# Seven block products for w_out times g, from batch 4 on

## The chip, the cores and the metric

The kernel runs on one core of one Trainium2 chip. That core has five engines with a queue each: TensorE (PE in the profile; its weight loads are listed apart as PEld), VectorE (DVE), ScalarE (ACT), GpSimd (POOL) and SyncE (SP), which here issues nearly all DMAs. An engine works off its own queue strictly in the order in which the program was written out, and waits at an instruction until the semaphores that it names are there. The metric is the device time of one execution in microseconds (us). The kernel before took 1190.68 us, the median of three runs (1190.14, 1190.68, 1194.91).

## What is computed

Two stages follow each other: attention with a sigmoid instead of a softmax, and a feed-forward layer on its output. With 8 batches of 12 heads, 448 positions and a head size of 64, cut to what matters:

```python
scores = scale * np.matmul(q, k.transpose(0, 1, 3, 2)) - np.log(S)
attn_out = np.matmul(1.0 / (1.0 + np.exp(-scores)), v)
x = attn_out.transpose(0, 2, 1, 3).reshape(3584, 768)
h = x @ w_in                                   # 768 x 2048
g = np.where(h >= 1, h, np.where(h <= -1, 0.0, (h + 1) ** 2 / 4.0))
out = g @ w_out                                # 2048 x 768
```

Everything arrives and leaves in float32.

## The kernel before, in words

**Precision.** TensorE is fed float16. Each float32 operand is scaled by a power of two and split into a high half (its float16 rounding) and a low half (what is left, again float16), and a product is the sum of three float16 matmuls: high times high, high times low, low times high. That is why every matmul loop has the inner loop `for wh, xh in ((0, 0), (0, 1), (1, 0))`.

**Stages.** The work goes batch by batch. For batch b there is an *up* stage (w_in times x, giving h, and from it g) and a *down* stage (w_out times g, giving the output). While the up and down stages of batch b run, the attention of batch b+1 is computed in small steps between them; batch 7, the last, has no attention beside it. Batch 0 and 1 also contain the loading, scaling and splitting of the weights.

**Up.** From batch 2 on, `up_blocks` computes h with seven products instead of eight of half-size blocks (a Strassen-type scheme): w_in, seen as 2 x 2 blocks, was combined once into seven blocks (`mix`, in batch 1, into the DRAM tile `blocks`), x is combined into seven blocks `xc` at the start of each batch, and seven products of 224 columns each are added up on VectorE into the four quarters of h. One index i stands for a pair of 128-row chunks of h, i and i + 8; there are eight of them, of 63 matmuls each. VectorE adds the quarters (L697, 128x224, five for each i); these additions also free the PSUM tiles in which the products stand.

**Bend.** `bend` turns a chunk of h into g: a Relu on ScalarE (L735), two operations on VectorE (L736, L737), the rounding to the high half on ScalarE (L738) and the low half on VectorE (L739). Each is 128x448, and there are two such chains for each i. The halves go to `ghl`.

**Down.** `down` multiplies the split w_out, which stays in SBUF as `w_out_sb`, by `ghl`: for each of six row chunks m, 16 chunks f times three matmuls of 448 columns (L758), 288 in all for a batch. VectorE scales the result out of PSUM (L768) and SP stores it (L770). From batch 2 on the f run in the order (0, 8), (1, 9), ..., so that the pair that the up stage finishes last is used last.

**What sets the order.** Python code emits the instructions unit by unit; `step` calls of the attention are spread evenly over the units of a batch. A scheduler then lists the instructions of each engine by priority and by its own estimate of when their operands are ready. What it wrote out is what the chip runs.

## Time and profile before

| | |
|---|---|
| median of 3 runs | 1190.68 us |
| the profiled execution's own time | 1187.38 us |
| its span (first to last instruction on the core) | 1185.7 us |
| granted TensorE clock, mean | 0.991 |
| TensorE busy | 1144.9 us (97%), 7662 matmuls |
| VectorE busy | 854.9 us (72%) |
| ScalarE busy | 697.6 us (59%) |
| GpSimd busy | 332.8 us (28%) |

Busy time is the time in which at least one instruction of the engine is under way. The up stage of batch b begins at about 394 us for batch 2, 532 for batch 3, 669 for batch 4, 806 for batch 5, 944 for batch 6 and 1078 for batch 7: a batch takes some 137 us, the last 108. In the timeline of an engine, instructions of one kind that follow each other are merged into one row with their count; in the table of groups each row has the mean duration of one. A duration includes the time in which the result drains, which the next instruction of the same engine overlaps if it doesn't depend on it.

### The profile page before, as it was taken

The page shows a single profiled execution, that of the slowest core. Times are in us where ns is not written, and L with a number is a line of the kernel's source. Part 1 is how long each engine was busy: PE and PEld are TensorE (multiplying, and loading weights), DVE is VectorE, ACT ScalarE, POOL GpSimd, SP SyncE. Part 2 cuts the span into 40 slices and gives each one's busy share as a digit, 9 for nine tenths or more (in the row PEclk, how much of TensorE's full clock was granted, in tenths as well). Part 3 has the DMA queues.
Part 4 walks back from the last instruction along what each step waited for, and adds up shares of the span by engine and source line. Part 5 has one row for each costly group of instructions (what it writes and reads, how often), then busy time and mean ns, then how long its engine had stood idle before and what let it go on. Part 6 is the DMA issues. An engine that isn't in the chain of part 4 may idle for free.

```text
span 1185.7 us, 20268 instructions
## 1 busy us (share of the span) xinstructions
PE 1144.9 (97%) x7662; PEld 669.3 (56%) x7662; DVE 854.9 (72%) x1828; ACT 697.6 (59%) x1158; POOL 332.8 (28%) x393
## 2 busy tenths in 40 slices
PE   5889899999999999999999999999999999999998
PEld 1224333444445776457754677557764577558954
DVE  6999999999956588457973689456884678736830
ACT  5886576665654577547864578455864476613510
POOL 3004410011323244234345235332532353310000
PEclk9899999999999999999999999999999999999999
DMA  9842354437542266224643065423552246302400
GB/s 367 322 153 76 118 161 152 134 119 257 182 148 72 95 217 210 76 72 142 238 163 102 30 236 208 135 64 128 204 211 64 65 147 220 126 24 87 163 16 32
DMA packets 58113, 170.01 MB, mean 143 GB/s; under 512 B 8608, under 2 KB 39840, under 8 KB 51872
## 3 DMA queue, kind: packets, MB, share of 16 engines
q1 hardware_dynamic: 56288, 159.29, 39.1%
q10 hardware_dynamic: 1728, 9.44, 2.2%
...
## 4 chain that ended last, share of the span: by engine, by line
PE 71%; DVE 17%; DMA 4%; ACT 3%; issue 2%; POOL 2%; SPq 0%; POOLq 0%; ACTq 0%; DVEq 0%
PE po L758 33%; PE ph L688 22%; PE pav L498 8%; PE psc L416 3%; PE psc L425 2%; PE ph L722 2%; DVE g L736 2%; PE psc L411 1%; DVE g L737 1%; DVE ghl L739 1%; DMA raw<-qkv 1%; DVE ahl L466 1%; DVE w_in_sb L244 1%; DVE mixa L632 1%; DVE w_out_sb L247 1%
## 5 line engine op out<-in xcount | busy, mean ns | idle before, releaser
L758 PE MATMUL po<-ghl,w_out_sb 128*128 128x448 f16 x2304 | 446.3, 353 | 1.5 <-DVE qkv_e L131 0.6
L758 PEld LDWEIGHTS <-w_out_sb 128*128 128x128 f16 x2304 | 221.7, 98 | 219.4 <-issue 15.9
L688 PE MATMUL ph<-w_in_sb 128*128 128x224 f16 x3024 | 307.7, 259 | 1.3 <-DVE g L737 0.9
L688 PEld LDWEIGHTS <-w_in_sb 128*128 128x128 f16 x3024 | 282.6, 98 | 30.1 <-issue 27.2
L466 DVE SCALAR_TENSOR_TENSOR ahl<-psc,ahl 128x896 f16<-128x896 f32 (+1 forms) x170 | 153.0, 900 | 105.7 <-ACT ahl L465 103.6
L378 POOL TENSOR_SCALAR raw<-raw,qkv_s 128x448 f32<-128x448 f32 (+1 forms) x93 | 71.0, 777 | 449.9 <-DVE qkv_i L139 346.3
L457 ACT ACTIVATE psc<-psc,nls,sqk 128x896 f32<-128x896 f32 (+1 forms) x136 | 129.5, 971 | 103.5 <-PE psc L425 86.6
L465 ACT ACTIVATE ahl<-psc 128x896 f16<-128x896 f32 (+1 forms) x170 | 126.9, 762 | 29.8 <-DVE ahl L466 28.6
L722 PE MATMUL ph<-xhl,w_in_sb 128*128 128x448 f16 x576 | 114.5, 356 | 4.7 <-DVE g L737 3.4
L344 ACT ACTIVATE dump<-raw 128x448 f16<-128x448 f32 (+1 forms) x105 | 61.9, 589 | 85.8 <-DMA raw<-qkv 84.5
L697 DVE TENSOR_TENSOR xhl<-ph,xhl 128x224 f32<-128x224 f32 x240 | 87.7, 383 | 25.3 <-PE ph L688 19.4
L738 ACT ACTIVATE ghl<-g 128x448 f16<-128x448 f32 x128 | 72.5, 573 | 44.2 <-DVE g L737 43.8
L498 PE MATMUL pav<-ahl,v 128*64 128x448 f16 x748 | 95.6, 360 | 0.0
L735 ACT ACTIVATE g<-xhl,hr,ihr 128x448 f32<-128x448 f32 x96 | 68.7, 752 | 41.9 <-DVE xhl L697 41.0
L722 PEld LDWEIGHTS <-w_in_sb 128*128 128x128 f16 x576 | 55.7, 99 | 63.6 <-issue 14.4
L736 DVE SCALAR_TENSOR_TENSOR g<-g,rk 128x448 f32<-128x448 f32 x112 | 81.4, 741 | 10.2 <-ACT g L735 10.0
L739 DVE TENSOR_TENSOR ghl<-g,ghl 128x448 f16<-128x448 f32 x128 | 85.0, 672 | 5.3 <-ACT ghl L738 4.8
L768 DVE TENSOR_SCALAR o<-po,od 128x448 f32<-128x448 f32 x48 | 32.5, 679 | 61.1 <-PE po L758 60.8
L380 POOL TENSOR_TENSOR hl<-raw,hl 128x448 f16<-128x448 f32 x62 | 71.1, 1167 | 0.0
L416 PE MATMUL psc<-qk 128*128 128x448 f16 x252 | 66.3, 354 | 2.0 <-ACT a L454 1.0
L737 DVE SCALAR_TENSOR_TENSOR g<-xhl,ihs,g 128x448 f32<-128x448 f32 x96 | 66.3, 708 | 0.3
L498 PEld LDWEIGHTS <-v 128*64 128x64 f16 x748 | 36.3, 109 | 37.9 <-issue 23.0
...
## 6 DMA issues: line engine op xcount, KB each, us to landing
w_in_sb<-blocks SPq DMA_DIRECT2D x48, 1344.0 KB, 6.1
...
```

What stands on the lines that cost most here:

```text
L416: nc.tensor.matmul(out, kq[:, j, 1, w], kq[:, j, 0, :], start=True, stop=False)
L457: nc.scalar.activation(a, a, AF.Sigmoid, bias=nls, scale=sqk)
L465: nc.scalar.activation(hi, x, AF.Copy, scale=ATT)
L466: nc.vector.scalar_tensor_tensor(out=lo, in0=x, scalar=ATT, in1=hi, op0=ALU.mult, op1=ALU.subtract)
L498: nc.tensor.matmul(pav[j * D : (j + 1) * D, :S], *terms[j][t], start=c == 0 and t == 0, stop=mid and t == len(terms[j]) - 1,)
L688: nc.tensor.matmul(out, w[:, wt, wh, c * P : (c + 1) * P], xc[:, xt, c, xh, :], start=j in (0, 2) and c + wh + xh == 0, stop=c == HC - 1 a ...
L697: add = lambda out, q, other: nc.vector.tensor_tensor(out=out, in0=quarter(q), in1=other, op=ALU.add)
L722: nc.tensor.matmul(ph[:, :S], w_in_sb[:, f, wh, c * P : (c + 1) * P], xhl[:, c, xh, :], start=c == 0 and wh + xh == 0, stop=c == NCC - 1 a ...
L736: nc.vector.scalar_tensor_tensor(out=g, in0=g, scalar=rt, in1=g, op0=ALU.min, op1=ALU.mult)
L737: nc.vector.scalar_tensor_tensor(out=g, in0=h, scalar=ihs, in1=g, op0=ALU.mult, op1=ALU.max)
L739: (nc.gpsimd if f % GPOOL else nc.vector).tensor_tensor(out=ghl[:, f, 1, :], in0=g, in1=hi, op=ALU.subtract)
L758: nc.tensor.matmul(po[:, :S], w_out_sb[:, f, wh, m * P : (m + 1) * P], ghl[:, f, gh, :], start=f == lo and wh + gh == 0, stop=f == hi - 1 ...
```

## The change

From batch 4 on (`SD = 4`) the down stage also uses seven products of half-size blocks.

- `mix_out` makes seven blocks from w_out, in eight pieces of two chunks each, with the same kind of arithmetic as `mix` (two sums and four combinations on VectorE, four roundings on ScalarE, four low halves and six rescalings on VectorE), and stores them in the DRAM tile `oblocks` by seven DMAs for each piece. It is emitted in batches 2 and 3.
- In the down stage of batch b >= 4 the blocks come back through a ring of six buffers of 512 KB each (128 x 2048 float16) that lie in the second part of `w_out_sb`, whose old contents aren't needed any more; one such load belongs to each product of 24 matmuls.
- `bend_blocks` takes the place of the two `bend` chains for an index i: Relu (128x896), two VectorE operations (128x896), four subtractions (128x224) that combine g into seven blocks, a rounding of 128x1568 on ScalarE and a low half of 128x1568 on VectorE. The blocks `gc` lie in the old `ghl` for i < 4 and in the first part of `w_out_sb` for i >= 4.
- `down_blocks` runs 3 x 7 products of eight chunks f times three matmuls of 224 columns, 504 in a batch, and adds the quarters of the result up on VectorE (L898 in the changed kernel, five for each m) and ScalarE.
- For m = 0 the first four products use the chunks f < 6 first (`ORD = 6`) and f = 6, 7 after that.
- Some constants move: four pairs of batch 7 have their largest values found by VectorE instead of ScalarE (`MAX_ACT` 47 to 43), two clamps of w_in in the first 30 us go from GpSimd to VectorE (`CLAMP`), two early loads are issued later (`L0`), the priority that the additions of the quarters get is smaller (`Q_PRIO` 72 to 12), and `mix` of w_in ends a little later (`MIX1`). Small tiles share buffers.

```diff
-MAX_ACT = 47
-L0 = 9
+MAX_ACT = 43
+L0 = 16
-CLAMP = 7
+CLAMP = 4
+SD = 4
+ORD = 6
+OMIX0 = 4
+OMIX1 = 96
+GP9 = 0
-MIX1 = 85
-Q_PRIO = 72
+MIX1 = 95
+Q_PRIO = 12
...
+    def mix_out(i):
...
+            (nc.gpsimd if r < MIXP else nc.vector).tensor_tensor(
+                out=a[:, r], in0=w_out_sb[:, chunk, 0, :], in1=w_out_sb[:, chunk, 1, :], op=ALU.add
+            )
+        a11, a21, a12, a22 = a[:, 0, :H], a[:, 0, H:], a[:, 1, :H], a[:, 1, H:]
+        nc.vector.scalar_tensor_tensor(out=a22, in0=a21, scalar=ratio, in1=a22, op0=ALU.mult, op1=ALU.add)
+        nc.vector.tensor_tensor(out=a21, in0=a11, in1=a21, op=ALU.subtract)
+        nc.vector.scalar_tensor_tensor(out=a11, in0=a11, scalar=minus, in1=a22, op0=ALU.mult, op1=ALU.add)
+        nc.vector.tensor_tensor(out=a12, in0=a12, in1=a11, op=ALU.subtract)
...
+        for t in range(4):
+            hi, scale = sv[:, t, :, 0, :], to[t != 1]
+            nc.scalar.activation(hi, src[:, t], AF.Copy, scale=scale)
+            nc.vector.scalar_tensor_tensor(
+                out=sv[:, t, :, 1, :], in0=src[:, t], scalar=scale, in1=hi, op0=ALU.mult, op1=ALU.subtract
+            )
...
+        for t in range(NB):
+            part = st[:, (t - 3) * DM : (t - 2) * DM] if t > 2 else pl[:, t * DM : (t + 1) * DM]
+            nc.sync.dma_start(
+                out=oblocks[:, t, :, i, :].rearrange("m p n -> p m n"), in_=part.rearrange("p (m n) -> p m n", m=HC)
+            )
...
-        if j == 6:
+        if j == 6 and b < SD:
             bend(b, i + NFC // 2, hg)
             bend(b, i, hf)
+        elif j == 6:
+            bend_blocks(b, i)
+
+    def bend_blocks(b, i):
...
+        nc.scalar.activation(g, h, AF.Relu, bias=hr, scale=ihr)
+        nc.vector.scalar_tensor_tensor(out=g, in0=g, scalar=rt, in1=g, op0=ALU.min, op1=ALU.mult)
+        nc.vector.scalar_tensor_tensor(out=g, in0=h, scalar=ihs, in1=g, op0=ALU.mult, op1=ALU.max)
+        sub = lambda o, x, y: nc.vector.tensor_tensor(out=t[:, o], in0=t[:, x], in1=t[:, y], op=ALU.subtract)
+        sub(4, 1, 0)
+        sub(1, 3, 1)
+        sub(5, 3, 4)
+        sub(6, 2, 5)
+        hi, lo = (gc[i][:, k].rearrange("p t n -> p (t n)") for k in range(2))
+        nc.scalar.activation(hi, blk, AF.Copy)
+        (nc.gpsimd if GP9 and i % GP9 == 1 else nc.vector).tensor_tensor(out=lo, in0=blk, in1=hi, op=ALU.subtract)
...
+    def down_blocks(b, m, j, lo, hi):
...
+        for f in range(lo, hi):
+            for wh, gh in ((0, 0), (0, 1), (1, 0)):
+                nc.tensor.matmul(
+                    out, w[:, f, wh, :], gc[f][:, gh, gt, :],
+                    start=j in (0, 2) and f + wh + gh == 0, stop=f == NHC - 1 and wh == 1, skip_group_check=True,
+                )
+        if hi < NHC:
+            return
+        load_block(n + RING)
...
+    def downs_blocks(b):
...
+        for m in range(HC):
+            late = 4 if m == 0 else 0
+            order += [(m, j, 0, ORD) for j in range(late)] + [(m, j, ORD, NHC) for j in range(late)]
+            order += [(m, j, lo, lo + NHC // 2) for j in range(late, NB) for lo in (0, NHC // 2)]
...
-        units = ups_blocks(b) + downs(b)
+        units = ups_blocks(b) + (downs(b) if b < SD else downs_blocks(b))
...
+                if 1 < b < SD:
+                    if b == 2 and u == 0:
+                        mix_scales(wo)
+                        omixed = 0
+                    v = (b - 2) * len(units) + u
+                    end = (SD - 3) * len(units) + OMIX1
+                    while omixed < NFC // 2 and v >= OMIX0 + omixed * (end - OMIX0) // (NFC // 2):
+                        mix_out(omixed)
+                        omixed += 1
```

How the scheduler's order moves is seen at three places.

**VectorE, start of batch 2's up stage.** `xhl<-ph` are the additions of the quarters, `ahl` the attention of the next batch, `xm` its maximum. Before:

```order
L697 TENSOR_TENSOR xhl<-ph,xhl 128x224
L466 SCALAR_TENSOR_TENSOR ahl<-psc,ahl 128x896
L508 TENSOR_REDUCE xm<-x_91 128x1
L697 TENSOR_TENSOR xhl<-ph,xhl 128x224 x2
L466 SCALAR_TENSOR_TENSOR ahl<-psc,ahl 128x896
L697 TENSOR_TENSOR xhl<-ph,xhl 128x224
L736 SCALAR_TENSOR_TENSOR g<-g,rk_3407 128x448
```

Now (`mixa`, `mixs` and `mixp` are tiles of `mix_out`):

```order
L711 TENSOR_SCALAR mixp<-w_out_sb,mixes 128x3x128 x6
L377 TENSOR_SCALAR sqk<-qkv_i 128x1
L378 TENSOR_SCALAR sqk<-qkv_i 128x1
L526 TENSOR_REDUCE xm<-x_91 128x1
L688 TENSOR_TENSOR mixa<-w_out_sb 128x768 x2
L484 SCALAR_TENSOR_TENSOR ahl<-psc,ahl 128x896
L765 TENSOR_TENSOR xhl<-ph,xhl 128x224 x3
L692 SCALAR_TENSOR_TENSOR mixa<-mixa,mixes 128x384
L765 TENSOR_TENSOR xhl<-ph,xhl 128x224
L693 TENSOR_TENSOR mixa<-mixa 128x384
```

The instructions of `mix_out` stand between the additions. Counted over the whole program, 70 of its 128 instructions on VectorE stand ahead of batch 2's first addition, beside the down stage of batch 1, and the other 58 between batch 2's first and last addition; none is left for the down stage of batch 2 or for batch 3.

**VectorE, end of batch 7's up stage.** Before, from the last two additions to the output:

```order
L697 TENSOR_TENSOR xhl<-ph,xhl 128x224 x2
L736 SCALAR_TENSOR_TENSOR g<-g,rk_11832 128x448
L736 SCALAR_TENSOR_TENSOR g<-g,rk_11822 128x448
L737 SCALAR_TENSOR_TENSOR g<-xhl,ihs_11836,g 128x448
L737 SCALAR_TENSOR_TENSOR g<-xhl,ihs_11826,g 128x448
L739 TENSOR_TENSOR ghl<-g,ghl 128x448 x2
L768 TENSOR_SCALAR o<-po,od 128x448 x6
```

Now:

```order
L765 TENSOR_TENSOR xhl<-ph,xhl 128x224 x2
L794 TENSOR_TENSOR blk<-blk 128x224
L801 TENSOR_TENSOR w_out_sb<-blk,w_out_sb 128x1568
L794 TENSOR_TENSOR blk<-blk 128x224 x3
L792 SCALAR_TENSOR_TENSOR blk<-blk,qm 128x896
L793 SCALAR_TENSOR_TENSOR blk<-xhl,ihs_12686,blk 128x896
L801 TENSOR_TENSOR w_out_sb<-blk,w_out_sb 128x1568
L794 TENSOR_TENSOR blk<-blk 128x224 x4
L801 TENSOR_TENSOR w_out_sb<-blk,w_out_sb 128x1568
L898 SCALAR_TENSOR_TENSOR u<-po,od,u 128x224 x2
```

After the last two additions there were six instructions until g was complete; now there are 13: a subtraction and the low half of i = 5, the rest of i = 6, and all of i = 7.

**VectorE, end of batch 4's up stage.** Before, from the last two additions to the last low half:

```order
L697 TENSOR_TENSOR xhl<-ph,xhl 128x224 x2
L736 SCALAR_TENSOR_TENSOR g<-g,rk_6844 128x448
L736 SCALAR_TENSOR_TENSOR g<-g,rk_6834 128x448
L737 SCALAR_TENSOR_TENSOR g<-xhl,ihs_6848,g 128x448
L737 SCALAR_TENSOR_TENSOR g<-xhl,ihs_6838,g 128x448
L156 CAST mb<-m_8178 128x3
L739 TENSOR_TENSOR ghl<-g,ghl 128x448 x2
```

Now, the last twelve rows up to the last low half:

```order
L792 SCALAR_TENSOR_TENSOR blk<-blk,qm 128x896
L153 TENSOR_SCALAR qkv_s<-qkv_e 128x3
L157 TENSOR_SCALAR qkv_i<-qkv_e 128x3
L801 TENSOR_TENSOR w_out_sb<-blk,w_out_sb 128x1568
L793 SCALAR_TENSOR_TENSOR blk<-xhl,ihs_7079,blk 128x896
L377 TENSOR_SCALAR sqk<-qkv_i 128x1
L378 TENSOR_SCALAR sqk<-qkv_i 128x1
L526 TENSOR_REDUCE xm<-x_91 128x1
L794 TENSOR_TENSOR blk<-blk 128x224
L484 SCALAR_TENSOR_TENSOR ahl<-psc,ahl 128x896 x2
L794 TENSOR_TENSOR blk<-blk 128x224 x3
L801 TENSOR_TENSOR w_out_sb<-blk,w_out_sb 128x1568
```

Ahead of these, behind the last two additions, stand three more subtractions, one `ahl` of 128x896 and one of 64x448, and two tiny ones. In batches 5 and 6 it reads alike. On TensorE, 30 matmuls of the down stage stand ahead of the last 18 of the up stage in each of batches 4 to 7, and 42 more of the chunks f < 6 behind them, before the first that needs f = 6.

More of the change, by code (lines that the diff above doesn't have):

```diff
@@ L123, in sigmoid_attention_mlp @@
     blocks = drm_p.tile([NFC // 2, P, SET], F16, name="blocks")
+    NHC = NFC // 2
+    GC, OB, RING = 2 * NB * HN, NHC * 2 * P, 6
+    gflat, oflat = (t.rearrange("p f h n -> p (f h n)") for t in (ghl, w_out_sb))
+    gc = [gflat[:, k * GC : (k + 1) * GC] for k in range(NHC // 2)]
+    gc += [oflat[:, k * GC : (k + 1) * GC] for k in range(NHC // 2)]
+    gc = [t.rearrange("p (h t n) -> p h t n", h=2, t=NB) for t in gc]
+    ring = [oflat[:, NHC // 2 * GC + k * OB : NHC // 2 * GC + (k + 1) * OB] for k in range(RING)]
+    ring = [t.rearrange("p (f h n) -> p f h n", f=NHC, h=2) for t in ring]
+    oblocks = drm_p.tile([HC, NB, P, NHC, 2 * P], F16, name="oblocks")
     def scales(m, n, tag, pool=None, square=False, less=0):
         pool = pool or sml_p
-        few = {"bufs": 1} if tag == "x" else {}
+        few = {"bufs": 1 if tag == "x" else 2} if pool is sml_p else {}
         mask, top = (EXP_MASK - EXP_ONE, TOP - 1) if square else (EXP_MASK, TOP - less)
-        e = sml_p.tile([P, 3], F32, tag="e", name=tag + "_e")[:, :n]
+        e = sml_p.tile([P, 3], F32, tag="e", name=tag + "_e", bufs=2)[:, :n]
         nc.vector.tensor_scalar(out=e, in0=m, scalar1=TINY, scalar2=None, op0=ALU.max)
@@ L617, in keep @@
             return t
-        low = keep("low", wi.scale[0], wi.scale[1], ALU.min, 0.25, ALU.mult)
-        keep("inv", wi.inv[0], wi.inv[1], ALU.max, 4.0, ALU.mult)
-        to = [keep("to%d" % k, low, wi.inv[k], ALU.mult) for k in range(2)]
-        keep("ratio", wi.scale[1], wi.inv[0], ALU.mult)
+        low = keep("low", w.scale[0], w.scale[1], ALU.min, 0.25, ALU.mult)
+        keep("inv", w.inv[0], w.inv[1], ALU.max, 4.0, ALU.mult)
+        to = [keep("to%d" % k, low, w.inv[k], ALU.mult) for k in range(2)]
+        keep("ratio", w.scale[1], w.inv[0], ALU.mult)
         keep("minus", mixed["ratio"], -1.0, ALU.mult)
@@ L649, in mix @@
         nc.sync.dma_start(out=blocks[i][:, 3 * DM :], in_=st)
[L650 removed]
+        pl = raw_p.tile([P, GC // 2], I32, tag="raww", name="mixp")[:, : 2 * DM].bitcast(F16)[:, : 3 * DM]
         pv = pl.rearrange("p (t h n) -> p h t n", t=3, h=2)
@@ L770, in down, with load_block, quarter @@
             nc.sync.dma_start(out=dst, in_=o)
+    OPRODUCTS = (0, 0, 0), (3, 5, 1), (4, 1, 2), (6, 4, 3), (1, 2, 0), (2, 6, 2), (5, 3, 3)
+    use = []
+    def load_block(n):
+        if n < HC * NB * (B - SD):
+            m, j = use[n % len(use)]
+            dst = ring[n % RING].rearrange("p f h n -> p (f h n)")
+            nc.sync.dma_start(out=dst, in_=oblocks[m, OPRODUCTS[j][0]].rearrange("p f n -> p (f n)"))
+    def down_blocks(b, m, j, lo, hi):
+        n = use.index((m, j)) + (b - SD) * HC * NB
+        if j % 2 == 0 and j < 4 and lo == 0:
+            hold["o", j] = ps_mo.tile([P, 512], F32, tag="mo", name="po")
+        if m == 0 and j == 0 and lo == 0:
+            hold["od"] = down_sc[b, None]()
+        if j == 0 and lo == 0:
+            hold["o"] = [out_p.tile([P, S], F32, tag="o", name="o%d" % r) for r in range(2)]
+            hold["u"] = tmp_p.tile([P, S], F32, tag="tmp", name="u")
+        wt, gt, q = OPRODUCTS[j]
+        def quarter(q):
+            return hold["o", q // 2 * 2][:, q % 2 * 256 : q % 2 * 256 + HN]
+        out, w = quarter(q), ring[n % RING]
+        for f in range(lo, hi):
[3 more added lines that the diff above has]
+                    start=j in (0, 2) and f + wh + gh == 0, stop=f == NHC - 1 and wh == 1, skip_group_check=True,
+                )
+        if hi < NHC:
+            return
+        load_block(n + RING)
+        o, od = hold["o"], hold["od"]
+        u2, u3 = hold["u"][:, :HN], hold["u"][:, HN:]
+        add = lambda out, q, other: nc.vector.scalar_tensor_tensor(
+            out=out, in0=quarter(q), scalar=od, in1=other, op0=ALU.mult, op1=ALU.add
+        )
+        with tc.high_priority(offset=Q_PRIO):
+            if j == 1:
+                nc.scalar.activation(u2, quarter(0), AF.Copy, scale=od)
+                add(u2, 1, u2)
+            elif j == 3:
+                add(u3, 2, u2)
+                add(o[1][:, HN:], 3, u3)
+            elif j == 4:
+                nc.scalar.activation(o[0][:, :HN], quarter(0), AF.Copy, scale=od)
+            elif j == 6:
+                add(o[1][:, :HN], 2, u2)
+                add(o[0][:, HN:], 3, u2)
+        if j == 6:
+            for r in range(2):
+                row = (m + r * HC) * P
+                nc.sync.dma_start(out=out_t[row : row + P, b * S : (b + 1) * S], in_=o[r])
@@ L901, in sigmoid_attention_mlp @@
         first = at
-        share = [DW if b < SB or u < len(units) - 48 else 8 for u in range(last)]
+        share = [DW if b < SB or u < len(units) - NDOWN else 8 for u in range(last)]
         share = [sum(share[:u]) / sum(share) for u in range(last + 1)]
@@ L924, in sigmoid_attention_mlp @@
                     block_scales(b + 1, inv_x)
+                if b == SD - 1 and u == len(units) - 1:
+                    downs_blocks(SD)
+                    for n in range(RING):
+                        load_block(n)
                 if b == 1 and u == last - 2:
```

65 lines of the change are left out of this document (49 added, 16 removed).

## The prediction

> **What bounds the kernel now.** First the page's busy times and slices:
>
> ```profile
> span 1185.7 us, 20268 instructions
> PE 1144.9 (97%) x7662; PEld 669.3 (56%) x7662; DVE 854.9 (72%) x1828; ACT 697.6 (59%) x1158; POOL 332.8 (28%) x393
> PE   5889899999999999999999999999999999999998
> DVE  6999999999956588457973689456884678736830
> ```
>
> TensorE is full from slice 5 on, so less matmul work shortens the run, as long as no other engine takes its place. VectorE is no flat 72%: it swings between 3 and 9 tenths inside each batch. So I cut the up stages out, from the first to the last addition of the quarters, for batches 2, 4 and 7, and then the last down stage (columns: stretch, its length, then busy us and instructions of each engine):
>
> ```profile
> core 0: us, PE busy (x) PEld busy (x) DVE busy (x) ACT busy (x) POOL busy (x), PEclk, DMA share, GB/s
> 397.50:469.00 71.50, 71.50 (x633) 54.61 (x632) 61.69 (x132) 54.44 (x97) 35.39 (x44) 1.00 0.55 191
> 671.80:743.90 72.10, 72.10 (x638) 55.04 (x636) 62.20 (x133) 54.70 (x98) 35.64 (x44) 1.00 0.55 190
> 1080.20:1132.40 52.20, 51.26 (x509) 48.59 (x508) 38.37 (x82) 22.41 (x45) 0.00 (x0) 1.00 0.36 134
> 1132.00:1185.70 53.70, 49.98 (x265) 25.64 (x262) 8.24 (x14) 2.56 (x4) 0.00 (x0) 1.00 0.07 26
> ```
>
> TensorE never idles in the two full batches, but VectorE has only 10 us to spare in 72: 61.69 of 71.50 and 62.20 of 72.10. The slack of VectorE lies in the down stages. The change takes work from TensorE in the down stages and gives work to VectorE in the up stages, where there is least room.
>
> **What TensorE saves.** Prices from batch 7, where nothing stands between the matmuls:
>
> ```profile
> 1100.59 25.19 PE L688 MATMUL ph<-w_in_sb 128*128 128x224 f16 x261 [0.94 <-DVE g L737]
> 1131.50 50.48 PE L758 MATMUL po<-ghl,w_out_sb 128*128 128x448 f16 x266
> ```
>
> A matmul of 448 columns takes 50.48 / 266 = 0.1898 us, one of 224 takes 25.19 / 261 = 0.0965 us. A down stage was 288 x 0.1898 = 54.7 us and becomes 504 x 0.0965 = 48.6 us: 6.0 us saved, in four batches **-24.1 us**.
>
> [...]
>
> **What VectorE gets.** Groups by shape (count, busy us, mean ns of one, idle before):
>
> ```profile
> L736 DVE SCALAR_TENSOR_TENSOR g<-g,rk 128x448 f32<-128x448 f32 x112 | 81.4, 741 | 10.2 <-ACT g L735 10.0
> L737 DVE SCALAR_TENSOR_TENSOR g<-xhl,ihs,g 128x448 f32<-128x448 f32 x96 | 66.3, 708 | 0.3
> L739 DVE TENSOR_TENSOR ghl<-g,ghl 128x448 f16<-128x448 f32 x128 | 85.0, 672 | 5.3 <-ACT ghl L738 4.8
> L697 DVE TENSOR_TENSOR xhl<-ph,xhl 128x224 f32<-128x224 f32 x240 | 87.7, 383 | 25.3 <-PE ph L688 19.4 <-ACT xhl L700 2.7 <-PE psc L159 2.7
> L632 DVE TENSOR_TENSOR mixa<-w_in_sb 128x768 f32<-128x768 f16 x16 | 14.7, 958 | 2.3 <-DMA blocks<-mixs 2.3
> L637 DVE SCALAR_TENSOR_TENSOR mixa<-mixa,mixes 128x384 f32<-128x384 f32 x8 | 4.9, 616 | 0.0
> L655 DVE TENSOR_SCALAR mixp<-w_in_sb,mixes 128x384 f16<-128x384 f16 x16 | 4.3, 314 | 0.0
> L466 DVE SCALAR_TENSOR_TENSOR ahl<-psc,ahl 128x896 f16<-128x896 f32 x102 | 110.7, 1085 | 97.8 <-ACT ahl L465 97.6
> L465 ACT ACTIVATE ahl<-psc 128x896 f16<-128x896 f32 x102 | 92.6, 913 | 0.6
> L738 ACT ACTIVATE ghl<-g 128x448 f16<-128x448 f32 x128 | 72.5, 573 | 44.2 <-DVE g L737 43.8
> ```
>
> *mix_out in batch 2.* The order puts 58 of its 128 VectorE instructions between batch 2's first and last addition: 6 of 128x768 (0.958), 13 combinations and 15 low halves of 128x384 (0.616) and 24 rescalings (0.314): 5.7 + 17.2 + 7.5 = 30.4 us; with one attention instruction fewer (1.085), 61.69 + 30.4 - 1.1 = 91.0 us of VectorE work. TensorE has 71.50 us there plus 17 matmuls of the down stage that moved ahead (17 x 0.19 = 3.2): 74.7. An in-order queue can't do 91 us of work in 74.7, and the additions that free the PSUM tiles stand behind the mix instructions, so TensorE waits: 16 us as the upper end. Durations contain drains which the next instruction overlaps (0.08 us each, by the pair of additions in the next fence: 0.69 for two of 0.383); 58 + some 50 existing ones take off 8.6. For the lower end, 4, some of the remaining lag is taken up behind the stretch, by the down matmuls that don't need the last chunks. I take **+10**, nearer to the sum without drains. The 70 instructions in the down stage of batch 1 cost nothing: VectorE has room there, and its cover is the 48 matmuls between two outputs; without it they would cost what the other 58 do.
>
> *bend_blocks.* An index i took 2 x (0.741 + 0.708 + 0.672) = 4.2 us of VectorE. By the slope from 448 to 768 columns (0.672 to 0.958, 0.9 ns each) an operation of 896 takes 1.14 and one of 1568 about 1.8; with four subtractions of 0.383: 2 x 1.14 + 1.5 + 1.8 = 5.6 us. In batches 4 to 6 the order leaves 10 us more of VectorE in the stretch: 62.2 + 10 = 72 against 74 on TensorE. That fits, barely; I take 0.5 us a batch, **+1.5** (0 to 6).
>
> *The end of the up stage.* This is where most is lost. Now, in batch 7 (TensorE as above: 18 matmuls end at 1131.66):
>
> ```profile
> 1131.70 0.69 DVE L697 TENSOR_TENSOR xhl<-ph,xhl 128x224 f32<-128x224 f32 x2 [2.41 <-PE ph L688]
> 1132.98 1.34 DVE L736 SCALAR_TENSOR_TENSOR g<-g,rk 128x448 f32<-128x448 f32 x2 [0.59 <-ACT g L735]
> 1134.23 1.27 DVE L737 SCALAR_TENSOR_TENSOR g<-xhl,ihs,g 128x448 f32<-128x448 f32 x2
> 1135.56 1.22 DVE L739 TENSOR_TENSOR ghl<-g,ghl 128x448 f16<-128x448 f32 x2
> ```
>
> g is complete 5.1 us after the last up matmul, under a down stage that can wait that long. In the changed order VectorE still has two additions (0.69), eight subtractions (8 x 0.34 with drains overlapped in part, 2.7), three low halves (5.4) and two operations of 896 (2.3), and waits for ScalarE's rounding of 1568 columns (0.573 + 1120 x 0.76 ns, the slope to L465's 913, = 1.4): 12.5 us. TensorE has 42 + 3 matmuls that don't need f = 7: 4.3 us. So it idles 8 us in batch 7, less if the low half of i = 5 starts before the last additions are due: **+7** (4 to 9). What was the saving of that batch is gone.
>
> In batches 4 to 6 VectorE's row is longer (three `ahl` of 1.085 and one of 64x448 come in: some 15.5 us), but TensorE has attention to do: 48 matmuls of 224 columns (4.6) and about 4.9 us of attention stand ahead of the first with f = 7. 15.5 - 9.5 = 6.0; some of it is the attention's own chain, which would run anyway, so I take 4.5 each (3 to 8): **+13.5**.
>
> *The rest.* The last addition pair is one addition longer than the single scaling before: **+0.4**. ScalarE: 54.7 of 72 us, and two chains become one: nothing. MAX_ACT moves four pairs' maxima to VectorE, under batch 5's and 6's down stage mostly; CLAMP and L0 touch the first 60 us, where VectorE gets two instructions and loses two waits: 0, within 2 us either way. Q_PRIO alone leaves batch 3's order as it was: 0.
>
> *The ring.* Each product of 24 matmuls (2.3 us) needs 512 KB.
>
> ```profile
> w_in_sb<-blocks SPq DMA_DIRECT2D x48, 1344.0 KB, 6.1
> ```
>
> At this row's 1344 KB in 6.1 us, 512 KB take 2.3 us, just the pace, with six buffers to smooth it: 0. If it is slower, TensorE waits in 84 products.
>
> **Sum.** -24.1 + 10 + 1.5 + 7 + 13.5 + 0.4 = +8.3 us. The profiled execution took 1187.38 us, 3.3 less than the median of the runs: 1187.4 + 8.3 + 3.3 = **1199 us**. All lower ends give -8.7 us (1182), all upper ends +33 (1224).
>
> **Rivals.** A change of 0.5% (6 us) is about what can be told from none.
>
> *Faster: the waits are hidden.* For it: TensorE kept on at full VectorE load in batch 1,
>
> ```profile
> 230.00:260.00 30.00, 27.55 (x137) 12.88 (x135) 29.66 (x64) 18.24 (x31) 4.67 (x3) 0.94 0.22 69
> 300.00:330.00 30.00, 29.64 (x165) 14.27 (x164) 29.80 (x52) 21.11 (x36) 10.77 (x11) 1.00 0.43 140
> ```
>
> losing 2.5 and 0.4 us in 30 with VectorE at 99%. If batch 2 costs 4, the ends of the up stages 2 in batches 4 to 6 and 2.5 in batch 7: -24.1 + 4 + 6 + 2.5 + 0.4 = -11 us, **1179 us**. Against it: there VectorE's demand equalled the time; in batch 2 it exceeds it. Chance 0.33.
>
> *No change.* The waits just eat the saving (7 + 10 + 6 + 1): **1190 us**, 0.17.
>
> *VectorE and GpSimd get in each other's way.* The longest and the usual low half (min/median/max ns) show it:
>
> ```profile
> L739 DVE TENSOR_TENSOR ghl<-g,ghl x128: 608/622/1572, 103.1 to 1136.2; 128x448 f16<-128x448 f32 x128
> ```
>
> If every instruction of bend_blocks (8 x 5.6 = 45 us) had to share its time with GpSimd's 35.6 us, a stretch would need 80 instead of 74 us: 4 to 6 us in each of batches 4 to 6, **1213 us**; the median at the minimum speaks for few such meetings. Chance 0.07. [...]
>
> *The ring comes late* in the down stages: at 2.6 us a load, 84 x 0.3 = 25 us, **1224 us**, 0.04.
>
> **Chances.** Forecast (slower, 1197 to 1209) 0.39. Faster 0.33, same 0.17, slower 0.39 + 0.07 + 0.04 = 0.50. Range 1176 to 1214, which leaves out the fast end of the faster case and the late ring; the forecast's own range is 1194 to 1209.
>
> **What would show it.** Right: down matmuls of 224 columns at 96 ns; VectorE above 95% in batch 2's up stage with TensorE waiting there some 10 us for additions (L765); gaps of TensorE ahead of L889 in four places, 4 to 8 us long, released by VectorE's L801 or ScalarE's L800; batch 3 as before. Wrong: TensorE without idle time in batch 2, or a first f = 7 matmul that follows at once.

## The result, and the profile after

The changed kernel takes **1264.0 us** (median of 4 runs, 1258.3 to 1265.6) against 1191.2 (1190.1 to 1194.9): 1.0597 times the time before, interval 1.0554 to 1.0639. The forecast was 1199, slower, with a range up to 1214: the sign was right, the size was not. The profiled execution took 1265.62 us, 78.2 more than the 1187.38 before.

Busy times and slices of the page, as shown of before in the prediction:

```profile
span 1263.9 us, 22469 instructions
PE 1161.5 (92%) x8526; PEld 757.4 (60%) x8526; DVE 988.6 (78%) x2008; ACT 724.2 (57%) x1126; POOL 351.6 (28%) x391
PE   4889899799989878999999999799888999799978
DVE  5999998898979989656873699657996579936951
PEclk9899899999989999999999999899998999999989
```

TensorE is no longer full: from slice 5 on there are holes of 1 to 3 tenths, most of them in slices in which VectorE shows 8 or 9, or just behind such, and its granted clock dips with some of them. To place the loss, both executions are cut at the first addition of the quarters in each batch's up stage (L697, now L765); the first row is all that lies ahead of batch 2's up stage, the last batch 7 to the end. Windows of before, with the columns of the prediction (stretch, length, busy us of TensorE, its weight loads, VectorE, ScalarE, GpSimd, then the granted clock):

```profile
0.00:397.50 397.50, 362.63 (x1827) 155.46 (x1828) 338.10 (x687) 254.62 (x394) 78.29 (x75) 0.97 0.49 169
397.50:534.90 137.40, 137.40 (x1023) 88.45 (x1022) 94.36 (x213) 86.81 (x151) 53.83 (x68) 1.00 0.42 143
672.10:809.40 137.30, 137.30 (x1025) 88.52 (x1023) 94.56 (x214) 86.73 (x152) 53.83 (x68) 1.00 0.42 143
809.40:947.30 137.90, 137.40 (x1023) 88.45 (x1021) 94.66 (x213) 86.66 (x151) 53.64 (x68) 1.00 0.42 143
947.30:1080.20 132.90, 132.12 (x985) 85.90 (x984) 92.43 (x195) 71.26 (x113) 39.09 (x46) 1.00 0.34 119
1080.20:1185.70 105.50, 100.84 (x770) 74.03 (x768) 46.23 (x94) 24.76 (x48) 0.00 (x0) 1.00 0.22 80
```

The same windows of the changed kernel (here with batch 3):

```profile
0.00:418.80 418.80, 373.76 (x1860) 159.56 (x1861) 375.32 (x766) 265.42 (x414) 77.69 (x73) 0.96 0.52 174
418.80:575.80 157.00, 142.66 (x989) 87.88 (x989) 122.56 (x273) 94.11 (x165) 56.34 (x68) 0.97 0.52 160
575.80:713.00 137.20, 137.20 (x1024) 88.52 (x1023) 93.76 (x206) 86.85 (x152) 54.21 (x68) 1.00 0.49 166
713.00:857.50 144.50, 136.40 (x1233) 108.35 (x1231) 113.42 (x229) 91.36 (x142) 59.83 (x69) 0.96 0.61 207
857.50:1010.80 153.30, 138.80 (x1239) 109.09 (x1237) 115.83 (x227) 84.93 (x123) 60.48 (x69) 0.97 0.59 200
1010.80:1151.30 140.50, 131.38 (x1181) 105.25 (x1179) 105.87 (x194) 73.27 (x96) 43.09 (x46) 0.98 0.55 187
1151.30:1263.90 112.60, 101.35 (x1014) 98.78 (x1012) 61.86 (x120) 28.30 (x37) 0.00 (x0) 0.97 0.47 158
```

Row by row: +21.3 before batch 2, +19.6 in batch 2, nothing in batch 3 (137.20, as before), then +7.2, +15.4, +7.6 and +7.1 in batches 4 to 7; together 78.2. So about half was lost before a single new product ran, where mix_out works and the changed constants act, and half in the four batches that were to save 24.1. In both halves VectorE's busy time is what grew: +37 and +28 us in the first two rows, some 19, 21, 13 and 16 in batches 4 to 7. In these four TensorE's busy time is as it was (507.9 us against 507.7), so the 24 saved came back in another form, and the time in which it is idle went from 5.9 to 43.0 us: that is the loss.

The up stages alone, first to last addition, of batches 2, 4, 5, 6 and 7:

```profile
418.80:511.20 92.40, 79.88 (x639) 56.65 (x639) 87.78 (x191) 63.43 (x113) 33.32 (x39) 0.96 0.66 206
713.00:792.40 79.40, 77.64 (x694) 58.84 (x692) 74.43 (x138) 59.00 (x89) 38.49 (x44) 1.00 0.55 197
857.50:942.40 84.90, 80.15 (x713) 60.70 (x710) 74.23 (x132) 56.80 (x86) 38.26 (x44) 1.00 0.56 196
1010.80:1093.60 82.80, 78.03 (x673) 57.25 (x670) 74.86 (x135) 52.80 (x68) 39.87 (x44) 0.98 0.48 168
1151.30:1205.10 53.80, 52.08 (x541) 51.60 (x540) 45.17 (x93) 21.57 (x28) 0.00 (x0) 1.00 0.44 157
```

Before, they were 71.5 us long in batch 2, 72.1 in batch 4 and 52.2 in batch 7 (the prediction's windows), with 62, 62 and 38 us of VectorE.

What TensorE waits for in batches 4 to 6 (713 to 1151.3 us) its groups show (count, busy us, mean ns of one, idle before and who ended it):

```profile
L756 PE MATMUL ph<-w_in_sb 128*128 128x224 f16 x1500 | 155.6, 260 | 3.7 <-DVE xhl L765 2.0 <-ACT xhl L774 1.6
L434 PE MATMUL psc<-qk 128*128 128x448 f16 x102 | 29.6, 364 | 10.3 <-DMA qk<-hl 9.2 <-DVE ahl L484 1.0
```

Of 31.7 us of such waits, 3.7 stand ahead of up products, for the quarters (L765, L774); 8.7 ahead of down products, for the last g (L800, L801); and 18.4, the most, ahead of the attention's matmuls, of which L434 is one. Before, it was 1.3 us in all.

The saving itself is there. The last down products (start, us, count; the first group takes 1.31 and the next starts 1.15 after it, so the pace is read from start to start):

```profile
1257.24 1.31 PE L889 MATMUL po<-ghl,w_out_sb 128*128 128x224 f16 x12
1258.39 1.31 PE L889 MATMUL po<-w_out_sb 128*128 128x224 f16 x12
```

12 matmuls of 224 columns in 1.15 us are 95.8 ns each; the 96.5 of the prediction stand, and 504 x 0.0958 = 48.3 us.

Last, the end of batch 7's up stage on TensorE (start, us, count, in brackets the idle time ahead and who ended it), and the clock there in windows of 2 us:

```profile
1202.05 1.89 PE L756 MATMUL ph<-w_in_sb 128*128 128x224 f16 x18
1205.06 0.35 PE L889 MATMUL po<-w_out_sb 128*128 128x224 f16 x2 [1.12 <-ACT w_out_sb L800]
1207.18 0.53 PE L889 MATMUL po<-w_out_sb 128*128 128x224 f16 x2 [1.77 <-DVE w_out_sb L801]
1207.51 2.45 PE L889 MATMUL po<-ghl,w_out_sb 128*128 128x224 f16 x12
...
1215.42 0.35 PE L889 MATMUL po<-w_out_sb 128*128 128x224 f16 x2 [2.09 <-ACT w_out_sb L800]
1217.24 3.14 PE L889 MATMUL po<-w_out_sb 128*128 128x224 f16 x16 [1.47 <-DVE w_out_sb L801]
```

```profile
1216.00:1218.00 2.00, 0.76 (x5) 0.60 (x5) 1.19 (x1) 0.00 (x0) 0.00 (x0) 0.82 0.00 0
1218.00:1220.00 2.00, 2.00 (x13) 1.56 (x12) 0.45 (x1) 0.45 (x1) 0.00 (x0) 0.50 0.62 135
1220.00:1222.00 2.00, 2.00 (x20) 1.86 (x18) 0.90 (x2) 0.00 (x0) 0.00 (x0) 0.83 0.84 305
```

The waits that were forecast are there, 6.45 us in all. What was not forecast comes behind them: 12 matmuls take 2.45 us, where 12 take 1.31 in the rows above, and 16 take 3.14, and the granted clock is at 0.50 meanwhile. Worked out from the three windows, an estimate, it stood there for some 3.4 us. The stretch ahead was not quite idle: two matmuls ran in it, between a wait of 2.09 us and one of 1.47.

### The profile page after: what moved, and what is told of

Its sections match the earlier page's. It is cut to its first block, busy times and chain, and to the rows that moved or that the text cites. A ratio compares the mean times of both kernels' runs of the same rounds, so it can differ in the third digit from the quotient of the medians.

```text
span 1263.9 us, 22469 instructions
## 1 busy us (share of the span) xinstructions
PE 1161.5 (92%) x8526; PEld 757.4 (60%) x8526; DVE 988.6 (78%) x2008; ACT 724.2 (57%) x1126; POOL 351.6 (28%) x391
## 5 line engine op out<-in xcount | busy, mean ns | idle before, releaser
L847 PE MATMUL po<-ghl,w_out_sb 128*128 128x448 f16 x1152 | 227.3, 355 | 1.0 <-DVE o L857 0.4
L396 POOL TENSOR_SCALAR raw<-raw,qkv_s 128x448 f32<-128x448 f32 (+1 forms) x93 | 85.5, 933 | 492.0 <-DVE qkv_i L157 313.8
L889 PEld LDWEIGHTS <-w_out_sb 128*128 128x128 f16 x2016 | 195.6, 100 | 28.9 <-issue 24.9
L847 PEld LDWEIGHTS <-w_out_sb 128*128 128x128 f16 x1152 | 110.6, 98 | 114.1 <-issue 14.6
L889 PE MATMUL po<-w_out_sb 128*128 128x224 f16 x1008 | 120.4, 268 | 15.1 <-DVE w_out_sb L801 7.6
L516 PE MATMUL pav<-ahl,v 128*64 128x448 f16 x748 | 110.4, 373 | 4.9 <-DVE ahl L484 2.5
L889 PE MATMUL po<-ghl,w_out_sb 128*128 128x224 f16 x1008 | 111.9, 261 | 0.9 <-DMA w_out_sb<-oblocks 0.9
L765 DVE TENSOR_TENSOR xhl<-ph,xhl 128x224 f32<-128x224 f32 x240 | 86.8, 382 | 15.0 <-PE ph L756 8.3
L362 ACT ACTIVATE dump<-raw 128x448 f16<-128x448 f32 (+1 forms) x93 | 54.8, 589 | 63.2 <-DMA raw<-qkv 59.3
L434 PE MATMUL psc<-qk 128*128 128x448 f16 x252 | 70.5, 362 | 22.2 <-DMA qk<-hl 11.5
L794 DVE TENSOR_TENSOR blk<-blk 128x224 f32<-128x224 f32 x128 | 58.5, 478 | 0.8
L425 PE MATMUL psc<-ghl 64*128 64x448 f32 (+1 forms) x128 | 37.9, 680 | 22.4 <-ACT a L472 18.0
L898 DVE SCALAR_TENSOR_TENSOR o<-po,od,u 128x224 f32<-128x224 f32 x36 | 15.1, 447 | 48.5 <-PE po L889 47.7
```

Of the source, the lines that this page charges most:

```text
L396: nc.gpsimd.tensor_scalar(out=rt, in0=rt, scalar1=s[:, t : t + 1], scalar2=1.0, op0=ALU.mult, op1=ALU.mult)
L516: nc.tensor.matmul(pav[j * D : (j + 1) * D, :S], *terms[j][t], start=c == 0 and t == 0, stop=mid and t == len(terms[j]) - 1,)
L765: add = lambda out, q, other: nc.vector.tensor_tensor(out=out, in0=quarter(q), in1=other, op=ALU.add)
L794: sub = lambda o, x, y: nc.vector.tensor_tensor(out=t[:, o], in0=t[:, x], in1=t[:, y], op=ALU.subtract)
L847: nc.tensor.matmul(po[:, :S], w_out_sb[:, f, wh, m * P : (m + 1) * P], ghl[:, f, gh, :], start=f == lo and wh + gh == 0, stop=f == hi - 1 ...
L889: nc.tensor.matmul(out, w[:, f, wh, :], gc[f][:, gh, gt, :], start=j in (0, 2) and f + wh + gh == 0, stop=f == NHC - 1 and wh == 1, skip_g ...
```

## The experiments

Each is an edit of the changed kernel, beside runs of the kernel before, which took 1188.8 to 1190.9 us (medians) in the four groups in which they ran. Most have two runs. The changed kernel's own runs span 1258.3 to 1265.6 us, so a whole time within some 5 us of 1264 is not told apart from it; what is read below that comes from rows of the traces.

### The numbers alone

```diff
-SD = 4
+SD = 8
...
-                if 1 < b < SD:
+                if 1 < b < SD < B:
```

> The changed kernel with its numbers (MAX_ACT 43, L0 16, CLAMP 4, MIX1 95, Q_PRIO 12) and small buffers, but with w_out times g as full products in every batch and no mixing of w_out. The changed kernel's batch 2 begins its up stage 21.3 us later than before, of which 6.6 us are there by 330 us. If the numbers cost what is lost by 330 us: 1197 us. If they cost nothing, as the prediction had it (0, within 2 us), all the lag comes from the mixing of w_out: 1191 us.

Measured: 1195.3 us, 1.0034 times before (1.0017 to 1.0052). The first addition of batch 2 comes at 402.4 us instead of 397.5, and every later batch is as before within 1.5 us. So the numbers cost 4 to 5 us, not 0, all ahead of batch 2.

### mix_out without its arithmetic, and with it but without its queue

```diff
-            part = st[:, (t - 3) * DM : (t - 2) * DM] if t > 2 else pl[:, t * DM : (t + 1) * DM]
+            part = w_out_sb[:, f if t < 4 else g].rearrange("p h n -> p (h n)")[:, t % 2 * DM : (t % 2 + 1) * DM]
```

This is mix_no_waiting; no_mixing also drops all VectorE and ScalarE instructions of mix_out.

> The changed kernel with the arithmetic of mix_out left out: the blocks that go to DRAM are copied straight from w_out, the same number of bytes, so the later products read other numbers. Theory: mixing is what costs the 14.7 us from 330 us to batch 2's up stage and the 20.7 us inside it; without it batch 2's up stage takes 72 us again and begins 14 us earlier, 1264 - 35 = 1229 us. Rival: the order or the numbers cost that: above 1250 us.

> The changed kernel with all arithmetic of mix_out kept, but the blocks written to DRAM are copied from w_out, so that SyncE's queue does not wait for VectorE at L716 (37 us of waiting in the changed kernel, with loads of q, k, v queued behind). Theory V, the added VectorE work itself is the cost: 1258 to 1264 us. Theory Q, the queue that is blocked is the cost: about as without mixing, 1229 to 1238 us.

Measured: 1239.9 us and 1266.1 us. Window of no_mixing (batch 2):

```profile
412.80:550.00 137.20, 137.20 (x1024) 88.52 (x1023) 94.56 (x214) 86.81 (x152) 54.09 (x68) 1.00 0.42 143
```

Without the arithmetic, batch 2 is as before, and its up stage takes 72.5 us. It still starts late, at 412.8: the numbers bring 4.9 us of that, and the rest probably the edit itself, since the copies wait for nothing any more and are issued at 175 to 258 us, in the busiest part. In the first 330 us of mix_no_waiting TensorE has done 1345 matmuls, against 1392 in the changed kernel: 47 fewer (41 in no_mixing), some 8 to 9 us at 0.19. So the mixing costs more than the 24 us of the direct comparison, about 32, and the two runs differ only in the arithmetic: 26 us for VectorE's and ScalarE's work alone. The 8 to 9 us that mix_no_waiting lost early it made good later (batch 2's up stage is 84.4 us long instead of 92.4). So SyncE's queue plausibly has that share of the cost, and theory Q is wrong as the main cause. This is an inference over an edit that moved something else too. One part of it is in the changed kernel's trace: in batch 2's up stage VectorE stands idle for 4.1 us ahead of the sums of mix_out (L688) until a store to DRAM (`oblocks<-mixp`) has ended; in mix_no_waiting, where the stores read `w_out_sb`, it doesn't.

### mix_out held back to the down stages

```diff
...
+            z = mixes[:, 12:13]
+            nc.vector.tensor_scalar(out=z, in0=gate[:, 0:1], scalar1=0.0, scalar2=None, op0=ALU.mult)
+            nc.vector.tensor_scalar(out=w6, in0=w6, scalar1=z, scalar2=None, op0=ALU.add)
...
```

`gate` is an output of the same batch's down stage, `w6` the six scales: their values stay, but chunks can't start earlier. Two chunks are now emitted in batch 1's down stage and three each in those of batches 2 and 3.

> The changed kernel with the mixing of w_out held back to down stages: the scales of each of its eight chunks are made to depend on an output of a down stage (two chunks in batch 1, three each in batches 2 and 3). Theory V, mixing costs where VectorE has no room: batch 2's up stage back to 72.5 us, one batch-1 stretch with 18 us of mixing instead of 42; 1264 - 20 - 5 = 1239 us. Rival: the mixing costs wherever it stands, since VectorE's queue is in order and the attention is behind it: the down stages of batches 2 and 3 get longer by 5 to 10 us each, 1250 us or more.

Measured: 1248.4 us, 16 less. Windows of batches 2 and 3:

```profile
410.80:556.30 145.50, 141.15 (x1045) 90.25 (x1043) 127.54 (x268) 93.50 (x164) 58.06 (x68) 1.00 0.50 163
556.30:699.10 142.80, 137.81 (x1012) 87.19 (x1012) 124.91 (x258) 93.65 (x164) 58.55 (x68) 1.00 0.56 187
```

Batch 2's up stage is back at 72.5 us, as theory V has it, but three chunks cost 6 to 8 us in each of the two batches, behind the up stage, as its rival has it. VectorE was half free there before, so room on average is not enough; what stands behind the mix instructions in its queue, the attention above all, would be delayed by them, but no run takes that apart.

### The low halves left out: all, the last two, the first six

```diff
-        (nc.gpsimd if GP9 and i % GP9 == 1 else nc.vector).tensor_tensor(out=lo, in0=blk, in1=hi, op=ALU.subtract)
+        if i < 6: nc.vector.tensor_tensor(out=lo, in0=blk, in1=hi, op=ALU.subtract)
```

This is no_low_last2; no_low_first6 has `i >= 6`, no_low_half no such line.

> The changed kernel with VectorE's low half of the g blocks (L801, 8 of 1.8 to 2.2 us a batch) left out; the products with low halves read what stands in the buffer. Theory D, VectorE has more work than the up stages have time from batch 4 on, and its queue is late for the next stage: 14.4 to 16 us of VectorE a batch gone, the up stages back at 72 us and the waits ahead of the first products with f = 6 and 7 halved; 8 to 10 us a batch in batches 4 to 6 and 5 in batch 7, 1264 - 32 = 1232 us. Rival: the waits are set by ScalarE's rounding and the attention's own chain: 1254 us or more.

> The changed kernel without the low halves of the last two g indices (i = 6 and 7) of each batch from 4 on: 3.6 us of VectorE a batch; the products with these low halves read what stands in the buffer. Leaving out all eight made the kernel 48 us faster. Theory C, the chain behind the last up product is the cost: these two stand in it, so most of the 48 us comes back, 1264 - 36 = 1228 us or less. Theory D, VectorE is overloaded over the whole up stage: a quarter of the 48 us, 1252 us.

> The complement: the changed kernel without the low halves of i = 0 to 5, 10.7 us of VectorE a batch. Theory C: 1264 - 12 = 1252 us. Theory D: three quarters of the 48 us, 1228 us.

Measured: 1215.6 us without all eight (48 less), 1252.7 without the last two (11 less), 1224.8 without the first six (39 less). Windows of batches 4 to 7 without all eight:

```profile
709.20:842.80 133.60, 131.42 (x1232) 107.74 (x1231) 100.75 (x221) 91.21 (x142) 53.88 (x69) 1.00 0.66 223
842.80:980.50 137.70, 132.87 (x1239) 109.27 (x1237) 100.00 (x220) 84.98 (x123) 52.34 (x69) 0.99 0.65 223
980.50:1107.90 127.40, 126.87 (x1182) 104.08 (x1181) 91.47 (x184) 72.73 (x96) 38.63 (x46) 1.00 0.62 206
1107.90:1212.00 104.10, 97.37 (x1013) 96.79 (x1011) 50.29 (x112) 27.85 (x37) 0.00 (x0) 0.99 0.51 171
```

These four are now 10.8 us faster than before (502.8 against 513.6). This run leaves out work that the result needs, so it is no gain to be had; it shows what these 60 us of VectorE's work in the four batches cost. The parts add up (11 + 39 = 50) and go nearly with the number of instructions (2 to 6): theory D, not theory C. And they act in different places: without the first six, batch 5's up stage is 72.4 us long instead of 84.9; without the last two it is still 84.0, and batches 4 and 7 get some 5 us shorter behind theirs.

The waits tell more. Without the first six, those of batches 4 to 6 fall from 31.7 to 12.0 us, those ahead of the attention's matmuls from 18.4 to 6.8, and L434 (707.4 to 1110.4 us) no longer waits for its loads:

```profile
L434 PE MATMUL psc<-qk 128*128 128x448 f16 x102 | 27.7, 355 | 4.5 <-DVE ahl L484 3.2 <-issue 1.2
```

That speaks against a rival: the 84 loads of the ring, 512 KB each, stand in the same queue as the attention's loads and could have made those late, but they are all still there in this run. It leaves another open. GpSimd makes part of the `hl` that these loads bring, and it too is relieved: it was busy 163.4 us in batches 4 to 6 of the changed kernel, 146.6 before and 144.9 without low halves. Whether the attention is late through VectorE or through GpSimd, no run tells.

### Less attention in the up stages

```diff
-DW = 8
+DW = 4
```

> The changed kernel with DW = 4 in place of 8: while a batch's up products are issued, the attention of the next batch moves forward half as fast, and the rest of it is issued with the down products. Theory D, VectorE is overloaded in the up stages and has room in the down stages: an up stage of batches 4 to 6 loses some 8 us of attention work on VectorE, its queue is no longer late, and each of the three batches comes back to some 139 to 141 us; 1264 - 18 = 1246 us or less. Rival: it is the chain behind the last up product that costs, and with less attention to stand ahead of it the waits grow: 1260 us or more.

Measured: 1265.2 us. Batch 5's up stage and what follows up to batch 6's:

```profile
859.30:935.40 76.10, 71.31 (x663) 57.25 (x661) 67.04 (x124) 48.96 (x72) 33.26 (x33) 1.00 0.55 193
935.40:1012.00 76.60, 67.63 (x602) 54.44 (x600) 47.47 (x104) 35.66 (x51) 30.69 (x35) 0.93 0.64 216
```

The up stage lost 7.2 us of VectorE and 8.8 of its length, and the stretch behind it grew by as much. Theory D's 1246 is missed by 19 us: the bare sum of VectorE's work in the up stage is not the bound. The rival has the number, but not its reason: the waits for the last g in batches 4 to 6 did not grow (5.8 us, 8.7 with DW = 8), while those ahead of the attention's matmuls did (20.6, 18.4). Attention brings work for both engines; moved away, it leaves VectorE's share of TensorE's time about where it was (67.04 to 71.31 here, 74.23 to 80.15 with DW = 8), while a low half left out lowers it (60.03 to 71.39 without the first six). That this share is what counts is a reading, not shown.

### The numbers of before, and three edits together

The five numbers back to those of before (old_numbers), and that with DW = 4 and the mixing in the down stages (all_dw4).

> The changed kernel with the five numbers as before (MAX_ACT 47, L0 9, CLAMP 7, MIX1 85, Q_PRIO 72). The numbers alone cost 0.34% with full products, seen by 402 us. If that adds up with the rest: 1264 - 4 = 1260 us. If the numbers suit the blocks (they were set together): above 1264 us.

> The three edits together: DW = 4, mixing held back to down stages, the five numbers as before. If the three costs add up: 1264 - 18 - 25 - 4 = 1217 us. If the down stages cannot take both the attention and the mixing: 1235 us or more.

Measured: 1259.5 us and 1246.7 us. Without the changed numbers the kernel is 4.5 us faster, as with full products, but within the spread of the changed kernel's own runs; the three together bring 17, the 16 of the mixing and little else.

### The last rounding in pieces, and matmuls that keep TensorE at work

```diff
...
+        if i >= 6:
+            half(0, 1)
+            sub(4, 1, 0)
+            sub(5, 3, 4)
+            half(4, 6)
+            sub(1, 3, 1)
+            half(1, 4)
+            sub(6, 2, 5)
+            half(6, 7)
...
```

`half(a, b)` rounds blocks a to b - 1 and makes their low halves.

> The changed kernel with the rounding of the last two g indices cut in four pieces of 1, 2, 3 and 1 blocks, in the order in which the first products need them; the first product then needs only the first block, ready some 4 us after the last addition instead of some 12. Theory C: the waits ahead of the first f = 6 and 7 matmuls go from some 6 to 10 us a batch to 2 to 4, and the clock stays up behind them: 6 to 9 us a batch, 1264 - 30 = 1234 us. Theory D: six more instructions for VectorE a batch, 1264 us or somewhat more.

Measured: 1259.5 us. Batch 7 has what theory C wants (108.0 us instead of 112.6). Its waits, on TensorE, in the pieces run:

```profile
1206.17 0.35 PE L901 MATMUL po<-w_out_sb 128*128 128x224 f16 x2 [1.12 <-ACT w_out_sb L797]
1208.29 0.35 PE L901 MATMUL po<-w_out_sb 128*128 128x224 f16 x2 [1.77 <-DVE w_out_sb L798]
1208.48 1.31 PE L901 MATMUL po<-ghl,w_out_sb 128*128 128x224 f16 x12
...
1213.43 0.26 PE L901 MATMUL po<-w_out_sb 128*128 128x224 f16 x1 [0.57 <-ACT w_out_sb L797]
1213.91 0.64 PE L901 MATMUL po<-w_out_sb 128*128 128x224 f16 x5 [0.23 <-DVE w_out_sb L798]
...
1217.13 1.31 PE L901 MATMUL po<-ghl,w_out_sb 128*128 128x224 f16 x12
```

Five waits of 0.2 to 0.6 us with matmuls between them leave the clock at 1.00, and the next 12 matmuls run at full pace. But the first two waits, 1.12 and 1.77 us with two matmuls between, are those of the changed kernel to the hundredth; there the next 12 matmuls took 2.45 us at a clock of 0.50, here 1.31 at 1.00. So the length of the waits alone does not decide on the clock, and this run doesn't show that it was the cutting that kept it up. In batches 4 to 6 the edit gave nothing (145.5, 159.4, 137.9 us): of 30.5 us of waits there, 17.4 stand ahead of the attention's matmuls, nearly as many as without the edit.

```diff
+            for k in range(40 if (m, j) == (0, 0) and f >= ORD else 0):
+                nc.tensor.matmul(
+                    hold["o", 0][:, HN : HN + 32], w[:, 0, 0, :], gc[0][:, 0, 0, :32],
+                    start=False, stop=False, skip_group_check=True,
+                )
```

> The changed kernel with 40 matmuls of 32 columns, whose results nobody reads, ahead of the first product's f = 6 and again ahead of its f = 7 in each batch from 4 on, so that TensorE does something in the gap in which it waits for VectorE. In the changed kernel the granted clock goes to 0.50 for some 10 us behind each gap, 3.3 to 3.9 us of matmul time a batch. If the idle time causes that: the clock stays at 1.00 there in batch 7 and the whole gives back up to 3 us a batch, 1252 to 1258 us. If the clock falls anyway: the added matmuls cost up to 4 us a batch and the clock is 0.50 behind the gap as before, 1264 to 1280 us.

Measured: 1264.5 us, no change. In batch 7 the added matmuls were over before the wait began: they stood ahead of the waiting one and took 1.16 us each time, the waits behind them were 0.58 and 1.19 us, and the clock still went to 0.50. Whether work inside the gap would keep the clock up is not settled by this run, nor by the pieces.

### Half of the low halves on GpSimd

```diff
-GP9 = 0
+GP9 = 2
```

> The changed kernel with GP9 = 2: the low halves of i = 1, 3, 5, 7 are computed by GpSimd instead of VectorE. Amount theory: 7 to 8 us a batch less for VectorE in the up stages; by the runs without low halves (50 us for 59 us of VectorE work) 4 x 7.4 x 0.83 = 25 us, less some 3 us a batch for a slower last index: about 1250 us. Sharing theory: GpSimd's subtraction of 128x448 takes 1.2 us, so one of 1568 some 4 us, 16 us a batch in which VectorE's instructions with two SBUF inputs wait; nothing is won, 1262 us or more.

Measured: 1284.0 us, 20 more. Batch 7 is the clean case, since no attention is left for GpSimd there. Groups of VectorE and GpSimd from 1151.3 us on, in the changed kernel (count, busy us, mean ns of one, idle before):

```profile
L794 DVE TENSOR_TENSOR blk<-blk 128x224 f32<-128x224 f32 x32 | 11.6, 384 | 0.2
L801 DVE TENSOR_TENSOR w_out_sb<-blk,w_out_sb 128x1568 f16<-128x1568 f32 x4 | 7.1, 1784 | 1.6 <-ACT w_out_sb L800 1.6
```

and in the run with GpSimd, from the same time on:

```profile
L794 DVE TENSOR_TENSOR blk<-blk 128x224 f32<-128x224 f32 x32 | 14.4, 472 | 0.3
L801 POOL TENSOR_TENSOR w_out_sb<-blk,w_out_sb 128x1568 f16<-128x1568 f32 x2 | 6.4, 3203 | 20.6 <-ACT w_out_sb L800 13.4 <-issue 7.2
L801 DVE TENSOR_TENSOR w_out_sb<-blk,w_out_sb 128x1568 f16<-128x1568 f32 x2 | 4.9, 2436 | 2.4 <-ACT w_out_sb L800 2.4
```

VectorE's instructions with two inputs in SBUF got 23 to 37% longer in three groups (these two, and L793 from 1144 to 1486 ns) and stayed as they were in a fourth (L792, 1142); over the whole program its busy time did not fall but rose, from 988.6 to 991.8 us, with 16 instructions of 1.8 us fewer. That is the sharing theory. In the changed kernel itself it shows in batch 4 (from 713 to 860 us), between two instructions of one shape, of which the second reads PSUM:

```profile
L794 DVE TENSOR_TENSOR blk<-blk 128x224 f32<-128x224 f32 x32 | 16.1, 522 | 0.2
L765 DVE TENSOR_TENSOR xhl<-ph,xhl 128x224 f32<-128x224 f32 x43 | 15.7, 383 | 1.6 <-PE ph L756 1.4
```

522 ns against 383, and 384 in batch 7 without GpSimd. Instruction by instruction: of the 168 of `bend_blocks` on VectorE in batches 4 to 6 (L792 to L794, L801), 45 take over 8% longer than their like in batch 7, 19.6 us more in all, and every one of the 45 overlaps an instruction of GpSimd; of the 120 additions (L765) 52 overlap one, and none takes longer than 393 ns. Another 29 of the 168 overlap one and are not longer by that measure; what tells them from the 45 is not shown.

### What could be put together

Mixing in the down stages, the numbers of before, and the rounding in pieces for i = 7 only.

> Three edits together: mixing held back to down stages (16 us alone), the five numbers as before (4 us alone) and the rounding of the last index cut in four pieces (4.7 us in batch 7 alone in the run with two indices cut). If they add up: 1264 - 16 - 4 - 5 = 1239 us, still 4% above the kernel before, since the up stages of batches 4 to 6 keep their VectorE work. If the rounding in pieces pays in batches 4 to 6 too: 1230 us or less.

Measured: 1236.7 us, 1.0406 times before (1.0373 to 1.044). The findings add up (1239 was expected), and batch 7 takes 108.3 us. But batches 4 to 6 keep their VectorE work (143.6, 147.8 and 138.7 us), and no version of this change that was tried beats the kernel before.

## Why the prediction was right or wrong

**Right: what TensorE saves.** 95.8 ns a matmul against 96.5; without the low halves it is seen in the whole time (10.8 us faster in four batches, of 24.1, since part of the waits remains). Each of these matmuls has a weight load of its own (8526 of each in the run, 47 loads in 4.51 us among the last down products), and 12 pairs of load and matmul take 1.15 us. The ring holds its pace: TensorE waited 0.9 us in all for its loads. But that was no matter of 2.3 us a load: a load of 512 KB took a median of 5.1 us to land, and the six buffers covered it. Batch 3 is as before.

**Right in mechanism: the end of the up stage.** Four places, released by L800 and L801, 15.1 us of direct waits in all: 6.45 in batch 7 where 7 were taken, 8.7 in batches 4 to 6 where 13.5 were. What failed is that a wait was priced as a wait: a lower clock came behind it. In each of batches 4 to 7 the granted clock was 0.50 for 6.8 to 10.2 us, which made the matmuls under way there take 3.3 to 3.9 us longer; in the kernel before, it was 1.00 throughout these batches. In batch 7 the balance is -6.0 (saving) + 6.4 (idle time) + 3.3 (clock) and some 3.4 that no row names; forecast +1.4, measured +7.1.

**Wrong, the largest: "that fits, barely; I take 0.5 us a batch".** An index was priced at 5.6 us and measures 5.5 of busy time in batch 7, but 6.3 to 6.4 in batches 4 to 6, where GpSimd works. So the stage holds 74 to 75 us of VectorE work instead of 72, and then some more for the last index behind it. That is as much as the 74 us that were counted for TensorE. Whatever waits for VectorE's in-order queue is then late: 39 us went with the first six low halves, where the term had 1.5. The wait that the step had in mind, of the up products for their additions, is the small one, 3.7 us in batches 4 to 6. The large one, 18.4 us ahead of the attention's matmuls, stands in no term. And the amount in the stage is not all of it, since with DW = 4 the stage had 7.2 us less and nothing was won. The rival in which VectorE and GpSimd get in each other's way, 0.07, had this cause and its size for VectorE (some 7 us a batch), but was argued away by a median that stood near the minimum. The few long ones, 45 of 168, make the mean.

**Wrong: mix_out, +10 taken, 36 measured** (21.3 - 4.9 + 19.6). VectorE was busy 87.8 us in batch 2's up stage, where 82.4 were counted on (91.0 less 8.6 of drains). Of these 8.6, 4 for the 50 existing instructions had been taken off already, since 61.69 is busy time, in which an overlap counts once (0.08 us for the pair of additions, 0.69 for two of 0.383); and the rescalings took 0.40 us instead of 0.314. VectorE waited another 4.6, of which 4.1 for a store that had to free a buffer: the upper end, 16, was nearer and even it was short of 20.7. The 70 instructions in batch 1's down stage were put at 0, "VectorE has room there"; the stretch ahead of batch 2 grew by 16.4 beyond the numbers, of which some 6 are 33 matmuls done ahead of time. Room on average was no cover there either: three chunks held back to a down stage still cost 6 to 8 us.

**Wrong: the numbers**, 0 taken within 2, 4 to 5 measured (4.4 by the medians, 4.9 by the traces).

**Where the sum went.** Of 70 us too little: 26 mix_out, 5 the numbers, 39 batches 4 to 7 (+37.3 measured against -1.7). The sign was forecast right, but the two terms that decide it, mix_out and bend_blocks, were far too small.

**Open.** The spread of the first addition of batch 2 between runs of the same instructions up to there (416.8 to 422.4 us), so that parts of less than 5 us in the first 400 us are not told apart; how mix_out's cost divides between VectorE's work and SyncE's queue; whether the low halves make the attention late through VectorE's time or through GpSimd's; what decides whether the clock falls behind a wait; and whether TensorE could be kept at full clock by work inside the gap.
